# A pad of 96 bytes instead of 32 at the top of on-chip memory, in a float32 kernel of linear attention, MLP and mixture of experts

## The chip, the core and the metric

The kernel runs on one core of a Trainium2 chip. The metric is the device time of one execution in microseconds. Before the change it is 2297.07 us, the median of three runs (2296.84 to 2305.61).

## What is computed

Three layers in a row, all in float32, on 4 sequences of 768 tokens with 8 heads of 48 values, so on 3072 tokens of 384 values:

```python
# 1. delta rule, token by token, for each sequence and head (48 x 48 state)
k_n = k / (norm(k) + 1e-6)
y[t]  = q[t] @ state
state = state + beta[t] * outer(k_n[t], v[t] - k_n[t] @ state)
# 2. MLP 384 -> 2048 -> 384
h = x @ w_in;  x = (h * tanh(softplus(h))) @ w_out
# 3. eight experts 384 -> 1024 -> 384, weighted by a matrix P
P = exp(x @ w_gate - max);  8 rounds: P /= row sums; P /= column sums; P *= N / E
out = sum over e of P[:, e] * (relu(x @ w1[e]) @ w2[e])
```

## The kernel before, in words

**Precision.** TensorE works on tiles of a reduced format, so each float32 operand is held as two tiles, a high part and a low part. A product takes three matmuls: high x high, low weight x high, high weight x low (`PASSES`, line 301).

**Two stages.** The first stage goes through six blocks of 512 tokens (`for c in range(NBLK)`, line 1465). In each block it interleaves many small attention matmuls with the matmuls of the MLP and of expert 0: `gemm1` (line 307) for the first products, `m_second` (line 1211) for the second product of the MLP, `e_second` (line 331) for the second product of expert 0. The weights of this stage live in six slots `w0` to `w5`. From the second block on they are read back from a DRAM copy (`wd`) that the first block wrote.

The second stage (line 1567 on) does experts 1 to 7. It makes three passes, `u` = 0, 1, 2, each over 1024 tokens. A pass has 28 steps: 7 experts times 4 groups of 256 hidden units. A step has 69 large matmuls. `first` (line 589) does 33 of them in seven groups `b` of 3 or 6; its moving operand is a slice of the tile `gx`, its weights are in one of three slots `gw`. `seconds` (line 652) does the other 36, for the step before; its moving operands are the tiles `gh` and `gl`, its weights are in the slot `gw` of the step before. The step's order is written out: one group `b`, then five matmuls of `seconds`, then the next group (lines 1620 to 1631). So the moving operand changes between `gx` and `gh`/`gl` fourteen times in a step. `drain` (line 596) adds each group's result to earlier ones on VectorE, `weigh` (lines 622 to 631) applies relu and the gate and splits into `gh` and `gl`. In pass 0 the weights are prepared; in passes 1 and 2 they are read back from DRAM (`again`, line 450). At the end of a pass `o_out` and `o_store` (lines 669 to 695) turn the result and write it; they interrupt the first three or four steps of the next pass with small matmuls (line 688).

**Where tiles lie.** Each partition of the on-chip memory (SBUF) is 229,376 bytes long, which is 448 times 512. A pool of tiles is laid from the bottom up, or, with `side="right"`, from the top down. The first pool on the right is the pad, a tile that nothing reads or writes:

```python
ctx.enter_context(tc.tile_pool(name="pad", bufs=1, side="right")).tile([128, 8], F32, name="pad")
```

Every right pool after it lies below it. The sizes of all the large tiles are multiples of 512 bytes, so all large tiles of one side have the same first byte mod 512. In the program as built before the change the slot `w4`, the first tile under the pad, ends 64 bytes below the top, so the pad of 32 bytes takes up 64. The first bytes are:

| tile | side | used as | first byte | mod 512 | mod 1024 |
|---|---|---|---|---|---|
| `gw0` to `gw2` | left | weights, second stage | 25984, 42368, 58752 | 384 | 384 |
| `gx` of passes 0 and 2 (`gxa`) | left | moving, `first` | 85376 | 384 | 384 |
| `gx` of pass 1 (`gxb`) | right | moving, `first` | 143296 | 448 | 960 |
| `gh`, `gl`, second stage | right | moving, `seconds` | 180160 on, in steps of 2048 | 448 | 960 |
| `w0` to `w5` | right | weights, first stage | 198592 and others | 448 | 960 |
| `xh`, `xl`, `gh`, `gl`, first stage | right | moving, first stage | 159680 and others | 448 | 960 |

A matmul's weights begin at a multiple of 512 bytes within their slot; its moving operand begins at a multiple of 2048 bytes within its tile (in line 331 alone the moving operand is a part of a weight slot). `kq`, `kt`, `us` and the other tiles of the attention matmuls are on the left side, at 384 mod 512 mostly.

Of the kernel before, what the change touches and what calls it, by code (L numbers as in the profile page):

```python
# [8 lines left out]
F32 = mybir.dt.float32  # L9
# [75 lines left out]
def delta_mish_sinkhorn_kernel(  # L85
# [18 lines left out]
    out_r = out.rearrange("(b s) d -> b s d", b=B)  # L104

    const = ctx.enter_context(tc.tile_pool(name="const", bufs=1))
    ctx.enter_context(tc.tile_pool(name="pad", bufs=1, side="right")).tile([128, 8], F32, name="pad")
    right = ExitStack()
    wpool = right.enter_context(tc.tile_pool(name="wpool", bufs=1, side="right"))
    rawp = ctx.enter_context(tc.tile_pool(name="rawp", bufs=2))  # L110
# [1456 lines left out]
    with tc.manual_schedule():  # L1567
# [5 lines left out]
        for s in range(N + 1):  # L1573
# [11 lines left out]
            side = {k: [] for k in range(7)}  # L1585
# [120 lines left out]
```

## Time and profile before

| | |
|---|---|
| median of three runs | 2297.07 us (2296.84 to 2305.61) |
| profiled execution, its own time | 2303.45 us |
| its span, first to last instruction | 2301.7 us |
| mean granted TensorE clock | 0.971 of full speed |
| TensorE matmuls busy | 2221.2 us, 97% of the span |
| VectorE, ScalarE, GpSimd busy | 1356.0, 648.2, 620.8 us |
| mean share of the DMA engines | 48.8% for the kernel's own queue |

The profile is one execution. Its engines are PE (TensorE's matmuls), PEld (its weight loads, which run beside the matmuls), DVE (VectorE), ACT (ScalarE), POOL (GpSimd) and SP (the queue that issues the DMAs). A matmul's recorded duration reaches into the next matmul, because matmuls are pipelined. So what a matmul costs in a dense row is the distance from its start to the next one's start, not its duration. In a merged row of n matmuls, the length is n - 1 such distances and one duration of about 0.39 us.

### The profile page before, as it was taken

How to read it: one execution, taken by the hardware profiler on the slowest of the kernel's cores; microseconds unless marked ns; L12 is line 12 of the kernel's file. 1: busy time of each engine (PE TensorE's matmuls, PEld its weight loads, DVE VectorE, ACT ScalarE, POOL GpSimd, SP SyncE). 2: the span in 40 equal slices, each digit the busy share in tenths (PEclk: the TensorE clock that was granted, in tenths of full speed). 3: DMA queues.
4: the chain of work that ended last, by engine and by line, in shares of the span. 5: the costliest groups of instructions: out<-in, count | busy, mean ns of one | idle time of the engine just before them, and what ended most of it. 6: DMA issues, size and time to landing. Idle time of an engine off the chain costs nothing.

```text
span 2301.7 us, 34912 instructions
## 1 busy us (share of the span) xinstructions
PE 2221.2 (97%) x14262; PEld 1817.4 (79%) x14262; DVE 1356.0 (59%) x2214; ACT 648.2 (28%) x1148; POOL 620.8 (27%) x488
## 2 busy tenths in 40 slices
PE   8788899999999999999999999999999999999998
PEld 6667788788888887788888887888888878888886
DVE  7894726336162134767767766666666666566665
ACT  6453331433323243233333321112112121111111
POOL 4504441432402153376776850000000000000000
PEclk7699999999999999999999999999999999999999
DMA  6385734646354477255555555443443444434342
GB/s 179 128 291 178 238 125 142 183 149 209 128 177 149 162 281 260 75 185 190 195 207 193 190 174 181 151 155 132 157 153 119 176 147 155 139 136 156 124 141 69
DMA packets 121103, 384.25 MB, mean 167 GB/s; under 512 B 9968, under 2 KB 46768, under 8 KB 120944
## 3 DMA queue, kind: packets, MB, share of 16 engines
q1 hardware_dynamic: 120944, 382.03, 48.8%
q8 instruction: 112, 1.84, 0.3%
q14 instruction: 47, 0.39, 0.0%
HBM read 290.14 MB, written 91.85 MB: 166 GB/s over the span
## 4 chain that ended last, share of the span: by engine, by line
PE 87%; DVE 8%; issue 2%; POOL 1%; DMA 1%; ACT 1%; SPq 0%; DVEq 0%; POOLq 0%; ACTq 0%
PE s L652 30%; PE b L589 28%; PE psh L307 11%; PE x L1211 7%; PE y L331 4%; DVE t L993 1%; DVE lane L999 1%; PE psa L930 1%; PE psa L1069 1%; DMA w<-wd 1%; PE psa L1125 1%; PE psa L1230 1%; PE psa L1091 1%; PE psa L1035 1%; DVE lane L963 1%
## 5 line engine op out<-in xcount | busy, mean ns | idle before, releaser
L589 PE MATMUL b<-gx,gw 128*128 128x512 f32 x2772 | 733.9, 393 | 0.1
L596 DVE TENSOR_TENSOR gt<-b,gt 128x512 f32<-128x512 f32 x588 | 398.4, 690 | 423.0 <-PE b L589 412.4
L589 PEld LDWEIGHTS b<-gx,gw 128*128 128x128 f32 x2772 | 519.4, 188 | 116.4 <-DVE gt L596 1.4
L652 PE MATMUL s<-gh,gw 128*128 128x512 f32 x2016 | 575.0, 394 | 1.4 <-ACT gh L628 1.4
L628 ACT ACTIVATE gh<-gt 128x512 fp32r<-128x512 f32 x336 | 212.3, 632 | 968.6 <-DVE gt L622 968.6
L652 PEld LDWEIGHTS s<-gh,gw 128*128 128x128 f32 x2016 | 378.8, 188 | 89.4 <-ACT gh L628 1.8
L307 PE MATMUL psh<-xh,w 128*128 128x512 f32 x864 | 287.8, 415 | 18.9 <-DVE gl L1200 8.4
L652 PE MATMUL s<-gl,gw 128*128 128x512 f32 x1008 | 301.1, 393 | 0.0
L622 DVE SCALAR_TENSOR_TENSOR gt<-gt,gp 128x512 f32<-128x512 f32 x336 | 284.9, 849 | 4.7
L652 PEld LDWEIGHTS s<-gl,gw 128*128 128x128 f32 x1008 | 189.7, 188 | 43.1
L307 PEld LDWEIGHTS psh<-xh,w 128*128 128x128 f32 x864 | 159.6, 194 | 61.8 <-DVE gl L1200 12.4
L1200 POOL TENSOR_TENSOR gl<-x,gh 128x512 fp32r<-128x512 f32 x80 | 103.0, 1288 | 380.6 <-ACT gh L1198 367.5
L631 POOL TENSOR_TENSOR gl<-gt,gh 128x512 fp32r<-128x512 f32 x112 | 165.8, 1488 | 132.5 <-ACT gh L628 70.0
L307 PE MATMUL psh<-xl,w 128*128 128x512 f32 x432 | 175.4, 406 | 0.4 <-DVE xl L786 0.4
L631 DVE TENSOR_TENSOR gl<-gt,gh 128x512 fp32r<-128x512 f32 x224 | 153.2, 684 | 35.2 <-ACT gh L628 35.1
L1211 PE MATMUL x<-gh,w 128*128 128x512 f32 x576 | 153.4, 403 | 0.0
L522 POOL TENSOR_TENSOR gx<-gxr,gx 128x768 fp32r<-128x768 f32 x18 | 33.4, 1858 | 377.9 <-ACT gx L521 376.6
L1211 PEld LDWEIGHTS x<-gh,w 128*128 128x128 f32 x576 | 110.6, 194 | 24.2 <-issue 0.3
L453 POOL TENSOR_TENSOR gw<-gr,gw 128x640 fp32r<-128x640 f32 x56 | 93.3, 1668 | 50.2 <-ACT gw L463 50.2
L307 PEld LDWEIGHTS psh<-xl,w 128*128 128x128 f32 x432 | 84.3, 195 | 21.2 <-DVE xl L786 2.1
L331 PE MATMUL y<-w,hh 128*128 128x384 f32 x384 | 99.3, 339 | 0.0
L1192 ACT ACTIVATE x<-psh 128x512 f32<-128x512 f32 x80 | 47.8, 597 | 144.2 <-PE psh L307 139.8
(196 smaller groups left out, 2271.4 us busy)
## 6 DMA issues: line engine op xcount, KB each, us to landing
w<-wd SPq DMA_DIRECT2D x120, 768.0 KB, 4.4
gw<-wg SPq DMA_DIRECT2D x56, 1280.0 KB, 8.0
gw<-wg SPq DMA_DIRECT2D x56, 768.0 KB, 5.1
wg<-gw SPq DMA_DIRECT2D x28, 1280.0 KB, 6.0
wg<-gw SPq DMA_DIRECT2D x28, 768.0 KB, 5.4
wd<-w SPq DMA_DIRECT2D x24, 768.0 KB, 4.9
gr<-in_w_dram SPq DMA_DIRECT2D x28, 384.0 KB, 3.3
raw<-in_w_dram SPq DMA_DIRECT2D x28, 384.0 KB, 4.0
```

The lines of the kernel that those rows point to most:

```text
L307: mm(ps, lhsT=wi(u, pw, kc), rhs=(xh, xl)[px][:, kc, :], start=(n == 0), stop=(n == 3 * KD - 1))
L331: mm(o[t], lhsT=(h, l)[ph][:, t * 128:(t + 1) * 128], rhs=wo(u, pw, 0, DM), start=(f == 0 and n == 0), stop=(f == U2 - 1 and n == 2))
L453: nc.gpsimd.tensor_tensor(out=w[:, 1, lo:hi], in0=r, in1=w[:, 0, lo:hi].bitcast(F32), op=ALU.subtract)
L589: mm(ps, lhsT=w[:, pw, i * 128:i * 128 + 128], rhs=x[:, px, j, :], start=(n == 0), stop=(n == last))
L596: add = lambda o, i: nc.vector.tensor_tensor(out=t[:, o], in0=ps, in1=t[:, i], op=ALU.add)
L622: nc.vector.scalar_tensor_tensor(out=t, in0=t, scalar=0.0, in1=pbs[u, e][:, o:o + 512], op0=ALU.max, op1=ALU.mult)
L628: nc.scalar.activation(out=h, in_=t, func=AF.Copy)
L631: return lambda: eng.tensor_tensor(out=l, in0=t, in1=h.bitcast(F32), op=ALU.subtract)
L652: mm(os[u][3 * half + d], lhsT=w[:, pw, at:at + 128], rhs=hids[s, z][ph], start=(start and new and n == 0), stop=(end and not new and n == 2))
L1192: nc.scalar.activation(out=mi_x[u % 2], in_=hps.pop(u), func=AF.Mish)
L1200: eng.tensor_tensor(out=l, in0=p, in1=h.bitcast(F32), op=ALU.subtract)
L1211: mm(x2ps[c][k], lhsT=wo(u, pw, k * 128, k * 128 + 128), rhs=(h, l)[pg], start=(f == 0 and n == 0), stop=(f == U1 - 1 and n == 2))
```

## The change

The pad has 24 values of 4 bytes per partition instead of 8:

```diff
     const = ctx.enter_context(tc.tile_pool(name="const", bufs=1))
-    ctx.enter_context(tc.tile_pool(name="pad", bufs=1, side="right")).tile([128, 8], F32, name="pad")
+    ctx.enter_context(tc.tile_pool(name="pad", bufs=1, side="right")).tile([128, 24], F32, name="pad")
     right = ExitStack()
     wpool = right.enter_context(tc.tile_pool(name="wpool", bufs=1, side="right"))
```

No instruction is added, removed or moved. Every tile on the right side begins 64 bytes lower. Tiles on the left side stay where they are.

## Rows read from the trace of the kernel before

**Rows 1.** The page: busy time of engines, then the chain that ended last.

```profile
PE 2221.2 (97%) x14262; PEld 1817.4 (79%) x14262; DVE 1356.0 (59%) x2214; ACT 648.2 (28%) x1148; POOL 620.8 (27%) x488
...
PE 87%; DVE 8%; issue 2%; POOL 1%; DMA 1%; ACT 1%; SPq 0%; DVEq 0%; POOLq 0%; ACTq 0%
```

**Rows 2.** Busy time by stretch: first stage, passes 0, 1, 2, tail.

```profile
core 0: us, PE busy (x) PEld busy (x) DVE busy (x) ACT busy (x) POOL busy (x), PEclk, DMA share, GB/s
0.00:935.20 935.20, 871.35 (x8388) 720.74 (x8389) 475.57 (x917) 328.01 (x651) 300.14 (x264) 0.93 0.55 183
935.20:1379.00 443.80, 441.22 (x1904) 356.40 (x1903) 314.08 (x420) 140.25 (x199) 307.72 (x217) 1.00 0.51 181
1379.00:1828.20 449.20, 447.06 (x1957) 366.15 (x1957) 280.61 (x437) 90.78 (x150) 12.89 (x8) 1.00 0.44 150
1828.20:2278.40 450.20, 448.18 (x1952) 364.00 (x1952) 277.33 (x430) 86.31 (x144) 0.00 (x0) 1.00 0.40 137
2278.40:2301.70 23.30, 13.34 (x66) 10.08 (x64) 8.40 (x14) 2.81 (x5) 0.00 (x0) 0.89 0.47 135
```

**Rows 3.** Waits that ended on TensorE's matmuls, 939 to 2278 us; total, times, longest.

```profile
PE of L688 <- ACT gf L675: 4.1, 2, 2.1
PE s L652 <- ACT gh L628: 1.4, 1, 1.4
PE sm L530 <- DVE gq L527: 1.1, 1, 1.1
```

**Rows 4.** Timeline: first group of steps 2 and 12 (pass 0); start, length, matmuls.

```profile
963.97 0.86 PE L589 MATMUL b<-gx,gw 128*128 128x512 f32 x3
...
1123.31 0.86 PE L589 MATMUL b<-gx,gw 128*128 128x512 f32 x3
```

**Rows 5.** Timeline: first group of steps 32 and 55 (pass 1).

```profile
1449.20 0.85 PE L589 MATMUL b<-gx,gw 128*128 128x512 f32 x3
...
1812.44 0.85 PE L589 MATMUL b<-gx,gw 128*128 128x512 f32 x3
```

**Rows 6.** Timeline: first group of steps 60 and 83 (pass 2).

```profile
1897.16 0.86 PE L589 MATMUL b<-gx,gw 128*128 128x512 f32 x3
...
2263.62 0.86 PE L589 MATMUL b<-gx,gw 128*128 128x512 f32 x3
```

**Rows 7.** Timeline of TensorE in the first stage, block 5, from the end of a line-331 row.

```profile
818.71 0.33 PE L331 MATMUL y<-w,hl 128*128 128x384 f32 x1
818.88 0.63 PE L307 MATMUL psh<-xh,w 128*128 128x512 f32 x2
...
820.96 0.61 PE L307 MATMUL psh<-xh,w 128*128 128x512 f32 x2
...
823.00 1.52 PE L1211 MATMUL x<-gh,w 128*128 128x512 f32 x6
...
827.08 1.52 PE L1211 MATMUL x<-gh,w 128*128 128x512 f32 x6
...
831.16 1.52 PE L1211 MATMUL x<-gh,w 128*128 128x512 f32 x6
```

**Rows 8.** Timeline: seven matmuls of the second stage's steps 0 and 1.

```profile
945.12 1.75 PE L589 MATMUL b<-gx,gw 128*128 128x512 f32 x7
```

**Rows 9.** All waits from 935 us on: TensorE's weight loads on VectorE's drain.

```profile
PEld b L589 <- DVE gt L596: 1.4, 4, 0.4
```

**Rows 10.** Waits of the DMA queue: reloads of weights in passes 1 and 2.

```profile
SPq L450 <- PE s L652: 681.9, 55, 14.7
```

**Rows 11.** DMA issues: count, size of each, median us to landing.

```profile
w<-wd SPq DMA_DIRECT2D x120, 768.0 KB, 4.4
...
gw<-wg SPq DMA_DIRECT2D x56, 768.0 KB, 5.1
```

**Rows 12.** Costliest groups: first products of the first stage, idle time and its enders.

```profile
L307 PE MATMUL psh<-xh,w 128*128 128x512 f32 x864 | 287.8, 415 | 18.9 <-DVE gl L1200 8.4 <-DMA w<-wd 5.2 <-ACT xh L1135 2.3
```

**Rows 13.** Busy time by stretch around the start of pass 1, as in Rows 2.

```profile
1391.80:1394.90 3.10, 0.95 (x5) 0.29 (x5) 1.89 (x4) 1.60 (x3) 0.00 (x0) 1.00 0.00 0
1395.65:1399.06 3.41, 3.41 (x9) 2.65 (x9) 1.89 (x4) 0.00 (x0) 0.00 (x0) 0.50 0.26 62
```

## The prediction

> **What bounds the kernel now.** I read the page's busy times first, then the busy times by stretch, then the waits of TensorE, and last the timeline, for the distance between matmuls. TensorE's matmuls are busy for 97% of the span and hold 87% of the chain that ended last [rows 1]. By stretch: the first stage takes 935 us; passes 0, 1 and 2 of the second stage take 443.8, 449.2 and 450.2 us, and in each TensorE is idle for no more than 2.6 us [rows 2]. In all of the second stage its matmuls waited 6.6 us for others, 4.1 of that at the two pass boundaries [rows 3]. So from 935 us on the time is the number of matmuls times the distance from one start to the next. The change can only matter through that distance, since it adds and removes no instruction.
>
> **The distance is not the same everywhere, and it goes with the first bytes.** All these matmuls stream 512 columns at the full clock.
>
> - Passes 0 and 2. Steps 2 to 12 take (1123.31 - 963.97) / 10 = 15.934 us each [rows 4], steps 60 to 83 take (2263.62 - 1897.16) / 23 = 15.933 us each [rows 6]. A step has 69 matmuls, so 230.9 ns each. Here the weights and `gx` lie at 384 mod 512, and `gh`, `gl` at 448.
> - Pass 1. (1812.44 - 1449.20) / 23 = 15.793 us [rows 5], 228.9 ns each. Here all moving operands lie at 448, the weights at 384.
> - First stage, where moving operands and weights all lie at 448. From 827.08 to 831.16 us there are 18 matmuls (9 of line 1211, 9 of line 307) in 4.08 us: 226.7 ns each; from 823.00 to 827.08 again 4.08 us [rows 7].
> - Steps 0 and 1 of the second stage, before `seconds` alternates with `first`: `gx` and the weights are both at 384, and seven matmuls take 1.75 us, so (1.75 - 0.39) / 6 = 226.7 ns [rows 8]. The level of the byte (384 or 448) is thus indifferent; what counts is whether both operands agree.
>
> Passes 0 and 2 do the same matmuls in the same order with different work on GpSimd, ScalarE and the DMA queue (pass 0 keeps GpSimd busy for 307.7 us, pass 2 for none [rows 2]) and agree to 1 ns per step. So the distance belongs to TensorE and its operands, not to a neighbour. My reading is that the stream of the moving operand and the load of the next weights disturb one another when they are out of step mod 512, and that every switch of the moving operand to another byte class starts the disturbance anew.
>
> **The change part by part.** The pad's 32 bytes took 64, either by rounding to 64 or by 32 bytes that are always left; by both, 96 take 128. So every right tile moves from 448 to 384 mod 512, where the left ones are. Then:
>
> - Pass 0: a step goes from 15.933 to 69 x 226.7 ns = 15.64 us, by 0.293 us. 27 steps (step 0 has no `seconds`) give 7.9 us.
> - Pass 1: from 15.793 to 15.64, by 0.153 us; 28 steps give 4.3 us.
> - Pass 2: 0.293 us in each of 28 steps gives 8.2 us.
> - Off this goes what stays disturbed. After a row of another kind the distance needs some nine matmuls to settle: line 307 after line 331 takes 820.96 - 818.88 = 2.08 us for nine, 0.04 more than the settled 2.04 (823.00 - 820.96) [rows 7]. Such interruptions in the second stage are the 16 outputs stored inside passes 1 and 2, and the four waits on VectorE [rows 9]: about 20 x 0.04 = 0.8 us. Today's distances hold part of that already, so I take 0.7.
>
> Sum: 7.9 + 4.3 + 8.2 - 0.7 = 19.7 us. Its bounds are 0 (the distance stays) and 20.4 us (settled everywhere).
>
> Edits at nothing, with their cover. In the first stage all large operands are on the right and move together, so they agree before and after; only the switch between left-side attention operands and right-side large ones changes its class. Its distances after a switch are already unsettled by the change of kind; bounded by the 0.04 us above on each of some 60 switches, both ways, it is -2.4 to +2.4 us, and I take 0. VectorE is busy for 314.1 of pass 0's 443.8 us, 71% [rows 2]; a step that is 1.8% shorter leaves it below 73%. The place where it is already late is the four waits of 1.4 us in all [rows 9]; each can grow by at most what a step gets shorter, 4 x 0.29 = 1.2 us. The reloads of weights wait for TensorE to free a slot, 681.9 us over 55 waits [rows 10]; if TensorE is earlier, so are they. DMAs into `w` begin at another byte: they land in 4.4 us, and the equally large ones into `gw`, at the byte to which `w` moves, in 5.1 us [rows 11], a different shape; if that 16% were the byte's doing, TensorE's 5.2 us of idle time on `w` [rows 12] would grow by 0.8 us. I take 0, since the landing is covered by the other slots.
>
> The profiled execution took 2303.45 us, 1.75 more than its span, and 6.4 more than the median. Against its own time the sum gives 2283.7. The median runs do the same matmuls, so the 19.7 us come off 2297.07 as well: 2277.4 us.
>
> **The rivals.**
>
> - Operands that are 512 bytes apart do not agree: the period is 1024. For the weights the rows speak against it: line 1211 alternates between weights at 448 and 960 mod 1024 and still runs at 226.7 ns [rows 7]. For the moving operand no row shows it. After the change `gx` of passes 0 and 2 is at 384 mod 1024, `gh` at 896. Then only pass 1 settles: 2297.1 - 4.3 = 2292.8 us.
> - The other side, slower: the same place, with a switch that costs more than today's. Today a switch costs 0.293 us / 14 = 21 ns. There are 14 x 56 = 784 switches in passes 0 and 2. If each cost the 40 ns of the switch from line 331 to line 307 [rows 7], that is 784 x 19 = +14.9 us, less 4.3 in pass 1: +10.6, so 2308 us. It decides from 21 + 4300 / 784 = 26 ns on. Against it: groups of 3 to 6 matmuls end before nine have passed.
> - The byte does nothing, and the passes differ for a reason I do not see: 2297 us. Pass 1 stands against pass 2 with the same work on all other engines, which leaves little but the place of `gx`.
> - The pad takes 96 bytes, not 128, so right tiles lie at 416: out of step as today, and equal to nothing on the left. Passes 0 and 2 would keep a switch of 32 bytes: 2290 to 2301 us.
>
> On the third: the Trainium skill, "TensorE: Matmul & The Clock Gate", section "Step-by-step: what each phase is for", says that TensorE has two independent read ports and that loading the next weights steals no read bandwidth from the running matmul. By that rule the place of an operand would be indifferent and the time would stay at 2297. The trace disagrees, with 226.7, 228.9 and 230.9 ns for the same kind of matmul.
>
> **How the numbers follow.** The forecast has 0.80: two independent places show 226.7 ns wherever the operands agree. The period of 1024 has 0.07, no effect 0.06, the misplaced pad 0.04, the costly switch 0.03. A measurement of this kernel can tell about 0.5%, 11.5 us, from no change. Only the forecast passes that, so faster has 0.80; slower has 0.03; the rest, 0.17, is within. Around the forecast the time can move by the -2.4 to +2.4 of the first stage, the 1.2 + 0.8 us of waits, and the clock: in pass 1's boundary TensorE sat idle and 0.75 us later ran 3.41 us at 0.50 of full speed, 1.2 GHz, with nine matmuls in place of fifteen [rows 13]; such a stretch costs 1.6 us and pass 2's boundary has none. That makes 2272 to 2283 for the likeliest alone. The range reaches on to the period of 1024: 2272 to 2293.
>
> **What would show it.** In the new trace the first groups of two steps, 23 apart, should lie 359.7 us apart (23 x 15.64) in pass 1 and in pass 2 alike, and the last group of pass 2 some 20 us earlier; the first stage should keep its 935 us. Steps of 15.64 us in pass 1 alone would show the period of 1024; steps over 15.93 us in passes 0 and 2, the costly switch; the same three numbers as now, no effect. A second stage that is shorter while the first is longer would make the time wrong with the steps right.

## The result, and the profile after

| | before | after |
|---|---|---|
| median | 2297.99 us (4 runs, 2296.84 to 2305.61) | 2276.33 us (4 runs, 2275.34 to 2281.22) |
| profiled execution, its own time | 2303.45 us | 2281.22 us |
| its span | 2301.7 us | 2279.4 us |

The ratio is 0.9903, with a 95% interval of 0.9877 to 0.9929: the kernel is 1.0% faster. The forecast was 2277.4 us.

The busy times by stretch, after (bounds of the stretch in us, then busy time and number of instructions of each engine, granted TensorE clock, share of the DMA engines, GB/s). The bounds are those of the same work as in [rows 2]: first stage, passes 0, 1 and 2, tail.

```profile
0.00:934.93 934.93, 871.67 (x8389) 721.59 (x8389) 476.86 (x917) 328.13 (x651) 300.76 (x264) 0.93 0.55 183
934.93:1370.58 435.65, 433.02 (x1903) 356.38 (x1903) 317.19 (x420) 140.30 (x199) 307.91 (x217) 1.00 0.51 185
1370.58:1814.03 443.45, 441.29 (x1958) 364.78 (x1956) 280.81 (x437) 90.86 (x150) 12.91 (x8) 1.00 0.45 152
1814.03:2256.10 442.07, 440.02 (x1952) 363.72 (x1951) 277.29 (x429) 86.30 (x144) 0.00 (x0) 1.00 0.41 140
2256.10:2279.40 23.30, 13.39 (x67) 10.19 (x65) 8.43 (x14) 2.99 (x6) 0.00 (x0) 0.85 0.47 135
```

Against [rows 2] the first stage keeps its time (935.2 and 934.9), pass 0 loses 8.15 us, pass 1 5.75, pass 2 8.13, and the tail nothing. With the 0.27 us of the first stage that is all of the span's 22.3 us. Those 0.27 us say little by themselves: the first matmul of `first` begins anywhere between 925.7 us (e7 below) and 937.7 us (e10) in the profiles, and between 925.7 and 934.9 us in the five kernels whose first stage is laid out alike (after the change, and e4 to e7). The steps of the second stage, which repeat to a few ns, therefore carry the argument, and not the whole times. The first groups of the same six steps as in [rows 4 to 6], in the timeline after (start, length, matmuls):

```profile
963.48 0.84 PE L589 MATMUL b<-gx,gw 128*128 128x512 f32 x3
...
1119.88 0.84 PE L589 MATMUL b<-gx,gw 128*128 128x512 f32 x3
...
1438.67 0.84 PE L589 MATMUL b<-gx,gw 128*128 128x512 f32 x3
...
1798.39 0.84 PE L589 MATMUL b<-gx,gw 128*128 128x512 f32 x3
...
1882.02 0.84 PE L589 MATMUL b<-gx,gw 128*128 128x512 f32 x3
...
2241.74 0.84 PE L589 MATMUL b<-gx,gw 128*128 128x512 f32 x3
```

(1119.88 - 963.48) / 10, (1798.39 - 1438.67) / 23 and (2241.74 - 1882.02) / 23 are all 15.640 us: all three passes now run at 226.7 ns a matmul, where they ran at 230.9, 228.9 and 230.9. In the costliest groups the mean recorded duration falls along with the distance, while the weight loads' stays at 188 ns:

```profile
L589 PE MATMUL b<-gx,gw 128*128 128x512 f32 x2772 | 725.7, 390 | 0.1
L652 PE MATMUL s<-gh,gw 128*128 128x512 f32 x2016 | 565.6, 389 | 1.4 <-ACT gh L628 1.4
L589 PEld LDWEIGHTS b<-gx,gw 128*128 128x128 f32 x2772 | 518.9, 188 | 108.6 <-ACT gt L598 1.3 <-issue 0.5
...
L652 PEld LDWEIGHTS s<-gh,gw 128*128 128x128 f32 x2016 | 378.3, 188 | 80.5 <-ACT gh L628 1.8
L652 PE MATMUL s<-gl,gw 128*128 128x512 f32 x1008 | 296.5, 389 | 0.0
```

### The profile page after: what moved, and what is told of

Its sections match the earlier page's. It is cut to its first block, busy times and chain, and to the rows that moved or that the text cites. A ratio compares the mean times of both kernels' runs of the same rounds, so it can differ in the third digit from the quotient of the medians.

```text
span 2279.4 us, 34912 instructions
## 1 busy us (share of the span) xinstructions
PE 2199.4 (96%) x14262; PEld 1816.7 (80%) x14262; DVE 1360.6 (60%) x2214; ACT 648.6 (28%) x1148; POOL 621.6 (27%) x488
## 4 chain that ended last, share of the span: by engine, by line
PE 87%; DVE 8%; issue 2%; DMA 1%; POOL 1%; ACT 1%; SPq 0%; DVEq 0%; POOLq 0%; ACTq 0%
PE s L652 30%; PE b L589 28%; PE psh L307 12%; PE x L1211 7%; PE y L331 4%; DVE lane L999 1%; DVE t L993 1%; PE psa L930 1%; PE psa L1069 1%; PE psa L1125 1%; DMA w<-wd 1%; PE psa L1091 1%; PE psa L1230 1%; DVE lane L963 1%; PE psa L1109 1%
## 5 line engine op out<-in xcount | busy, mean ns | idle before, releaser
L589 PE MATMUL b<-gx,gw 128*128 128x512 f32 x2772 | 725.7, 390 | 0.1
L652 PE MATMUL s<-gh,gw 128*128 128x512 f32 x2016 | 565.6, 389 | 1.4 <-ACT gh L628 1.4
L652 PE MATMUL s<-gl,gw 128*128 128x512 f32 x1008 | 296.5, 389 | 0.0
```

Source lines behind the costliest of these rows:

```text
L589: mm(ps, lhsT=w[:, pw, i * 128:i * 128 + 128], rhs=x[:, px, j, :], start=(n == 0), stop=(n == last))
L652: mm(os[u][3 * half + d], lhsT=w[:, pw, at:at + 128], rhs=hids[s, z][ph], start=(start and new and n == 0), stop=(end and not new and n == 2))
```

## The experiments

The theory, A: TensorE's distance between matmuls depends on the first byte of the moving operand against that of the weights, mod 512. Its rivals: B, the byte 384 is good by itself; C, what counts is how the other engines or the DMAs reach the right side; D, only the switch between unlike moving operands counts, and the weights' byte does not. No kernel leaves work out, and each differs from the kernel after the change in its pads alone. All but e1, which has four runs, were run once. Steps are read as above: first groups of steps 32 and 55 for pass 1, of steps 60 and 83 for pass 2, 23 steps apart. In kernels with added lines, the line 589 is 590 or 591. Every first byte given below is that of the program as built.

**1. Everything level at another byte (e1).** The pad is 32 bytes again; the left side is moved up instead.

```diff
-    ... tile_pool(name="pad", bufs=1, side="right")).tile([128, 24], F32, name="pad")
+    ... tile_pool(name="pad", bufs=1, side="right")).tile([128, 8], F32, name="pad")
+    ctx.enter_context(tc.tile_pool(name="lpad", bufs=1)).tile([128, 16], F32, name="lpad")
     rawp = ctx.enter_context(tc.tile_pool(name="rawp", bufs=2))
```

> The right side lies where it lay before the change (448 mod 512) and a pad of 64 bytes moves the large tiles of the left side from 384 to 448, so all large operands agree, at another byte than after the change. Theory A (the distance between matmuls depends on the difference between the first bytes of the moving operand and of the weights, mod 512): steps of 15.640 us in all three passes, time about 2276 us, 0.990 of before. Theory B (byte 384 is a good place for right-side tiles, by itself): passes 0 and 2 stay at 15.93, pass 1 at 15.79, time about 2297 us. Theory C (the gain came from moving the right side at all, e.g. from how VectorE, ScalarE, GpSimd or the DMAs reach it): as B.

2277.43 us against 2295.92 of before on the same chip: 0.9907 (0.9890 to 0.9925). Its timeline, pass 1 and pass 2:

```profile
1437.72 0.84 PE L590 MATMUL b<-gx,gw 128*128 128x512 f32 x3
...
1797.44 0.84 PE L590 MATMUL b<-gx,gw 128*128 128x512 f32 x3
...
1881.21 0.84 PE L590 MATMUL b<-gx,gw 128*128 128x512 f32 x3
...
2240.93 0.84 PE L590 MATMUL b<-gx,gw 128*128 128x512 f32 x3
```

359.72 / 23 = 15.640 us in both. The right side lies exactly where it lay before, and the gain is there. B falls, and of C what concerns the place of the right side.

**2. The weights alone out of step (e7).** In the second stage 64 bytes are put below the slots `gw` and 448 above, so that only `gw` changes its byte mod 512, to 448 (what lies above moves by 512); all moving operands stay at 384.

```diff
+        ctx.enter_context(tc.tile_pool(name="off64", bufs=1)).tile([128, 16], F32, name="off64")
         pool2["w"] = ctx.enter_context(tc.tile_pool(name="gw", bufs=1))
         gslots.extend(...)
+        ctx.enter_context(tc.tile_pool(name="off448", bufs=1)).tile([128, 112], F32, name="off448")
```

> As after the change, but the weight slots gw of the second stage alone lie 64 bytes higher, at 448 mod 512; all moving operands of the second stage stay at 384. Theory A (moving operand against weights): all three passes alike and like pass 1 before the change, 15.79 us a step, time about 2276 + 83 x 0.153 = 2289 us. Rival D (only the switch between moving operands of unlike bytes counts, the weights' byte is indifferent): 15.640 us in all passes, 2276 us.

2312.57 us, more than before the change. Pass 1 and pass 2:

```profile
1444.75 0.86 PE L591 MATMUL b<-gx,gw 128*128 128x512 f32 x3
...
1815.05 0.86 PE L591 MATMUL b<-gx,gw 128*128 128x512 f32 x3
...
1902.13 0.86 PE L591 MATMUL b<-gx,gw 128*128 128x512 f32 x3
...
2272.43 0.86 PE L591 MATMUL b<-gx,gw 128*128 128x512 f32 x3
```

370.30 / 23 = 16.100 us in both, 233.3 ns a matmul. D falls: the moving operands agree with one another, and the weights' byte alone costs 6.7 ns a matmul. But the size that A expected, 15.79, was wrong. It took 64 bytes below to cost what 64 above costs (228.9 - 226.7 = 2.2 ns, pass 1 before); they cost three times that. The mean duration of a weight load hardly moves, from 188 to 189 ns:

```profile
L591 PEld LDWEIGHTS b<-gx,gw 128*128 128x128 f32 x2772 | 520.8, 189 | 126.4 <-DVE gt L598 0.9 <-ACT gt L600 0.5 <-issue 0.5
```

**3. Differences of 128 and 256 (e2, e3).** Pads of 224 and 352 bytes.

```diff
-    ... .tile([128, 24], F32, name="pad")
+    ... .tile([128, 56], F32, name="pad")   # e2;  [128, 88] in e3
```

> The pad is 224 bytes, so right tiles lie at 256 mod 512, left ones at 384: a difference of 128. Theory A with a period of 512: steps longer than 15.640 us in all passes, about 15.79 in pass 1 and 15.93 in passes 0 and 2 if a difference of 128 costs what 64 costs. Rival, a period of 128: 15.640 us everywhere, time about 2276 us.

> The pad is 352 bytes, so right tiles lie at 128 mod 512, left ones at 384: a difference of 256. Theory A with a period of 512: steps longer than 15.640 us in all passes, about 15.79 in pass 1 and 15.93 in passes 0 and 2. Rival, a period of 256: 15.640 us everywhere, time about 2276 us.

e2 takes 2305.97 us, e3 2276.28. e2 in pass 1, then pass 2:

```profile
1445.88 0.85 PE L589 MATMUL b<-gx,gw 128*128 128x512 f32 x3
...
1814.66 0.86 PE L589 MATMUL b<-gx,gw 128*128 128x512 f32 x3
...
1899.50 0.85 PE L589 MATMUL b<-gx,gw 128*128 128x512 f32 x3
...
2265.95 0.86 PE L589 MATMUL b<-gx,gw 128*128 128x512 f32 x3
```

e3 in pass 1, then pass 2:

```profile
1433.78 0.84 PE L589 MATMUL b<-gx,gw 128*128 128x512 f32 x3
...
1793.50 0.84 PE L589 MATMUL b<-gx,gw 128*128 128x512 f32 x3
...
1877.13 0.84 PE L589 MATMUL b<-gx,gw 128*128 128x512 f32 x3
...
2236.85 0.84 PE L589 MATMUL b<-gx,gw 128*128 128x512 f32 x3
```

A difference of 128 gives 16.034 us in pass 1 and 15.933 in pass 2; a difference of 256 gives 15.640 in both. So A with a period of 512 falls: the period is 256, and not 128 or a part of it. In e2 a difference of 128 costs more than 64 above in pass 1, and the same as 64 above in pass 2.

**4. A difference of 192 below (e8).** If the period is 256, 192 below is 64 above, the kernel before. The pad is `[128, 72]`, 288 bytes.

> The pad is 288 bytes: right tiles lie at 192 mod 512, left ones at 384, so in pass 1 the moving operands lie 192 below the weights. Theory A with the period of 256 that the run with 256 suggests: 192 below is 64 above, so the steps are those of the kernel before: 15.793 us in pass 1, 15.933 in passes 0 and 2, time about 2296 us. Theory A with a period of 512 that happens to be harmless at 256: a length of its own, between 15.64 and 16.10 us, with no reason to equal 15.793 or 15.933.

2299.36 us. Pass 1, then pass 2:

```profile
1445.09 0.85 PE L589 MATMUL b<-gx,gw 128*128 128x512 f32 x3
...
1808.33 0.85 PE L589 MATMUL b<-gx,gw 128*128 128x512 f32 x3
...
1893.07 0.86 PE L589 MATMUL b<-gx,gw 128*128 128x512 f32 x3
...
2259.53 0.86 PE L589 MATMUL b<-gx,gw 128*128 128x512 f32 x3
```

363.24 / 23 = 15.793 and 366.46 / 23 = 15.933 us: the same two differences, to the last digit, as in [rows 5] and [rows 6]. The period of 256 is confirmed by two numbers that a period of 512 gave no reason to expect.

**5. Only gh and gl out of step (e6).** Below the pools of `gh` and `gl` the same two pads as in experiment 2, so these tiles alone lie at 320.

```diff
+        ctx.enter_context(tc.tile_pool(name="off64", bufs=1, side="right")).tile([128, 16], F32, name="off64")
         for i in range(2):
             pool2[i, "h"] = ...
+        ctx.enter_context(tc.tile_pool(name="off448", bufs=1, side="right")).tile([128, 112], F32, name="off448")
```

> As after the change, but the tiles gh and gl of the second stage alone lie 64 bytes lower, at 320 mod 512; gx and the weights stay at 384 in all passes. If it is the switch between unlike moving operands that lengthened passes 0 and 2: now all three passes are alike, at about 15.93 us a step, time about 2276 + 83 x 0.293 = 2300 us. If gh and gl do not matter: 15.640 us in all passes.

2306.31 us; all three passes are alike, at steps that alternate between 15.993 and 16.000 us. Pass 1, then pass 2:

```profile
1443.87 0.86 PE L591 MATMUL b<-gx,gw 128*128 128x512 f32 x3
...
1811.79 0.85 PE L591 MATMUL b<-gx,gw 128*128 128x512 f32 x3
...
1898.33 0.86 PE L591 MATMUL b<-gx,gw 128*128 128x512 f32 x3
...
2266.26 0.85 PE L591 MATMUL b<-gx,gw 128*128 128x512 f32 x3
```

367.92 / 23 and 367.93 / 23 are both 15.997. Passes alike, as expected; 0.06 above the 15.93, since `gh` and `gl` here lie 64 below the rest and not 64 above.

**6. Only gx of pass 1 out of step (e5).** The same two pads around the pool `gxb`.

> As after the change, but the gx tile of pass 1 alone lies 64 bytes lower, at 320 mod 512. Theory A: pass 1 alone loses its gain, at 15.9 to 16.1 us a step (in it the moving operand now switches between 64 below the weights and level with them); passes 0 and 2 stay at 15.640 us; time about 2276 + 28 x 0.36 = 2286 us. If the whole layout of the right side mattered (how many tiles agree with each other), passes 0 and 2 would change as well.

2288.87 us. Pass 1, then pass 2:

```profile
1436.31 0.86 PE L591 MATMUL b<-gx,gw 128*128 128x512 f32 x3
...
1804.31 0.86 PE L591 MATMUL b<-gx,gw 128*128 128x512 f32 x3
...
1889.71 0.84 PE L591 MATMUL b<-gx,gw 128*128 128x512 f32 x3
...
2249.43 0.84 PE L591 MATMUL b<-gx,gw 128*128 128x512 f32 x3
```

16.000 us in pass 1, 15.640 in pass 2. One tile out of step costs only in the pass whose matmuls read it.

**7. A large tile that TensorE does not read (e4).** The same two pads around `gt`, which VectorE, ScalarE and GpSimd read and write throughout the second stage.

> As after the change, but the tile gt alone lies 64 bytes lower, at 320 mod 512: VectorE, ScalarE and GpSimd read and write it, TensorE does not. Theory A: 15.640 us in all passes, time about 2276 us. Theory C (what counts is how the other engines' accesses fall beside TensorE's): steps longer than 15.640 us, towards 15.79 to 15.93.

2274.91 us; 15.640 us in pass 1 (1792.06 - 1432.34 = 359.72) and in the other passes:

```profile
1432.34 0.84 PE L591 MATMUL b<-gx,gw 128*128 128x512 f32 x3
...
1792.06 0.84 PE L591 MATMUL b<-gx,gw 128*128 128x512 f32 x3
```

The rest of C falls with it, as far as `gt` stands for the other engines' tiles.

**8. Differences of 32, above and below (e9, e10).** Pads of 64 and 128 bytes, `[128, 16]` and `[128, 32]`.

> The pad is 64 bytes: right tiles lie at 416 mod 512, left ones at 384, 32 above. If the distance grows with the difference (226.7 ns at 0, 228.9 at 64, 232.4 at 128): steps between 15.64 and 15.79 us in pass 1, about 15.72, and between 15.64 and 15.93 in passes 0 and 2; time about 2286 us. If only equal or unequal counts: 15.793 and 15.933 us as before, about 2296 us. If 32 bytes are too little to matter: 15.640 us, 2276 us.

> The pad is 128 bytes: right tiles lie at 352 mod 512, left ones at 384, 32 below. In pass 1 the steps so far: 15.640 us at a difference of 0 and 256, 16.100 at +32, 15.793 at +64 and -192, 16.035 at -128, and 16.100 with the weights 64 above. If only level operands are free of it, 32 below costs too: 15.8 to 16.1 us in pass 1, about 2295 to 2310 us. If there is a side on which a difference of 32 is harmless: 15.640 us, 2276 us.

2308.87 and 2316.18 us (before on the second one's chip: 2300.63). Pass 1 and pass 2 of e9, then of e10:

```profile
1443.28 0.86 PE L589 MATMUL b<-gx,gw 128*128 128x512 f32 x3
...
1813.58 0.86 PE L589 MATMUL b<-gx,gw 128*128 128x512 f32 x3
...
1900.17 0.85 PE L589 MATMUL b<-gx,gw 128*128 128x512 f32 x3
...
2268.78 0.85 PE L589 MATMUL b<-gx,gw 128*128 128x512 f32 x3
```

```profile
1452.64 0.86 PE L589 MATMUL b<-gx,gw 128*128 128x512 f32 x3
...
1822.93 0.86 PE L589 MATMUL b<-gx,gw 128*128 128x512 f32 x3
...
1909.56 0.85 PE L589 MATMUL b<-gx,gw 128*128 128x512 f32 x3
...
2276.18 0.85 PE L589 MATMUL b<-gx,gw 128*128 128x512 f32 x3
```

Pass 1 takes 16.100 us a step in both; pass 2 takes 368.61 / 23 = 16.027 in e9 and 366.62 / 23 = 15.940 in e10. For e9 all three expectations missed, for e10 pass 1 stands at the upper end of the first, whose 2310 us its time exceeds. So 32 bytes off are as bad as 64 below and worse than 64 above: the cost does not grow with the difference. The pad of 64 bytes also settles how the pad is laid: the right tiles then lie at 416, so 32 bytes are left at the top and the size is not rounded up to a multiple of 64.

All steps of pass 1 together, by how far the moving operands begin above the weights, mod 256:

| difference mod 256 | kernels | step, us | ns a matmul |
|---|---|---|---|
| 0 | after, e1, e3, e4 | 15.640 | 226.7 |
| 32 | e9 | 16.100 | 233.3 |
| 64 | before, e8 | 15.793 | 228.9 |
| 128 | e2 | 16.034 | 232.4 |
| 192 | e7 | 16.100 | 233.3 |
| 224 | e10 | 16.100 | 233.3 |

The best difference is the one that the change has: no kernel of these has a shorter step. Differences of 96 and 160, and any finer than 32, were not run.

Where only a part of the moving operands is out of step, the step is longer than the mean of the two distances by their share (33 matmuls of `first`, 36 of `seconds`). The second column says which tiles lie off the weights, and by how much:

| kernel, pass | out of step | mean by share, us | measured, us |
|---|---|---|---|
| before and e8, 2 | `gh`, `gl` by 64 | 15.720 | 15.933 |
| e2, 2 | `gh`, `gl` by 128 | 15.846 | 15.933 |
| e9, 2 | `gh`, `gl` by 32 | 15.880 | 16.027 |
| e10, 2 | `gh`, `gl` by 224 | 15.880 | 15.940 |
| e6, 2 | `gh`, `gl` by 192 | 15.880 | 15.997 |
| e5, 1 | `gx` by 192 | 15.860 | 16.000 |

So mixing them has a price of its own, 0.06 to 0.21 us in a step of fourteen changes from one to the other. How it comes about was not tried.

## Why the prediction was right, point by point

- **That TensorE alone bounds the second stage, through the distance between its matmuls:** right. The instructions are the same in number and order, and 22.0 of the 22.3 us gained lie in passes 0, 1 and 2.
- **The step of 15.640 us, taken from the first stage and from seven matmuls of steps 0 and 1:** right to the last digit in all three passes.
- **The terms:** pass 0 was to give 7.9 us and gave 8.15; pass 2 was to give 8.2 and gave 8.13. Pass 1 was to give 4.3 and gave 5.75. What it gave beyond is the clock, which the sum had left to the range: before, TensorE ran at half speed after the boundary [rows 13]; after, the six matmuls behind the same 2.1 us of idle time keep the full clock (the last line, a stretch in the form of [rows 13], has a granted clock of 1.00):

```profile
1385.78 0.81 PE L688 MATMUL of<-id_sb,gf 128*128 128x128 f32 x3 [2.12 <-ACT gf L675]
1386.35 1.64 PE L589 MATMUL b<-gx,gw 128*128 128x512 f32 x6
```

```profile
1385.00:1389.00 4.00, 3.17 (x15) 2.48 (x16) 1.64 (x4) 1.21 (x3) 0.00 (x0) 1.00 0.12 28
```

  Pass 1's first step went from 20.32 to 18.60 us, of which 0.15 is the distance. In e3 and e4, whose other steps are those of the kernel after the change, that step is long again, 19.93 and 19.99 us. So it is no part of the change: without it the profiled gain is 22.2 - 1.6 = 20.6 us; the forecast said 19.7. How many of the runs behind the medians have the stretch is not known.
- **The median itself, 2276.33 us for a forecast of 2277.4:** that it came within 1.1 us is in part luck. The first stage alone varies by 9 us between profiles of kernels that lay it out alike, and the range had no term for that. The range's lower end is also not what its terms give: 2277.4 - 2.4 - 1.6 = 2273.4, where 2272 is named.
- **The 0.7 us taken off for interruptions:** too much. The interrupted steps 29 and 30 went from 16.847 to 16.740 us and steps 57 and 58 from 16.960 to 16.740, which is 0.05 to 0.07 short of the clean steps' gain, some 0.25 us in all.
- **The four waits on VectorE's drain [rows 9], bounded at 1.2 us of growth:** wrong in sign. Steps 14 and 24 were 0.16 us longer than their neighbours before and are not any more; steps 12 and 22 still are, by 0.233 us. In the waits after, VectorE no longer stands among those that TensorE's loads for `first` waited on; ScalarE's copy does:

```profile
PEld b L589 <- ACT gt L598: 1.3, 3, 0.6
```

  Why two of them went was not tried.
- **First stage, reloads and DMAs at nothing:** borne out as far as one profile on each side can tell. 934.9 for 935.2 us, with the scatter named above, so the -2.4 to +2.4 us for its switches were neither shown nor excluded; transfers into `w` land in 4.4 us as before.
- **The rival of a period of 1024:** wrong, as forecast, and by more than was thought: the operands need to agree mod 256 only (e3, e8).
- **The rival of a costlier switch:** wrong. Passes 0 and 2 went down to 15.640 us and not up. Nor did a switch cost 21 ns: of the 0.293 us a step, 36 matmuls at 64 above account for 0.08, which leaves 0.21 us, or 15 ns a switch.
- **The rival that place does not matter:** wrong. The Trainium skill, "TensorE: Matmul & The Clock Gate", section "Step-by-step: what each phase is for", has the two reads of TensorE independent of one another. The measurement decides: e7 moves nothing but the weights, and every matmul of the second stage takes 233.3 instead of 226.7 ns.
- **The rival of a misplaced pad:** wrong; 96 bytes lay the right side at 384. Its price, 2290 to 2301 us, was too low: e9 is that layout, its steps are longer than before in all passes, and it takes 2308.87 us in its one run.
- **My reading of the mechanism:** right in its core, that what counts is the moving operand's byte against that of the weights (e7), and too simple. That it is the load of the next weights, beside the running matmul, which meets the moving operand is argued and not shown: the loads' recorded durations do not change. "Out of step mod 512" should have been mod 256, and what one pays depends on the difference, in no simple order. A switch of the moving operand is not needed for it: in pass 1 of e7, e9 and e10 nothing switches, and the steps are longer than any with switches. A switch does cost something besides, as the table of partly shifted kernels shows; that it "starts the disturbance anew" was not shown.

What stays open is which part of the chip has the period of 256 bytes, and how the six prices come about. The profile shows only that the weight loads keep their 188 to 189 ns while the matmuls' distance grows.

## What to carry to other kernels

Where dense matmuls follow one another without waits, compare the distance from start to start between stretches that do the same matmuls; a few ns apart, repeated to the digit, can point to where the operands lie. In this kernel, where every matmul has a weight load of its own and 512 columns, the best layout is the one in which the first bytes of moving operands and weights agree mod 256, across both ends of the on-chip memory; a pad of a few bytes does it, and the wrong one costs up to 3% of a step (16.100 for 15.640 us). Other shapes and types were not run. Check it by shifting one tile with a pad on one side and its complement to 512 on the other, so that everything else keeps its byte mod 512.

## What the runs showed of the hardware that was not expected

- The first byte of the moving operand against that of the weights costs between 0 and 6.7 ns a matmul of 512 columns at full clock, with a period of 256 bytes: 226.7 ns at 0, 228.9 at 64, 232.4 at 128, 233.3 at 32, 192 and 224.
- The cost is not symmetric (64 above: 228.9; 64 below: 233.3) and has what looks like a ceiling: three differences give 16.100 us on average over 23 steps.
- It is exact. Steps of one layout repeat to 1 ns in most layouts (in e2's pass 1, and in e6, e7, e9 and e10 neighbouring steps differ by some ns), beside different loads on GpSimd and the DMAs.
